# Reordering attention's norm and two in-place sums in a fused attention and feed-forward kernel

## The chip, the cores and the metric

The kernel runs on one core of one Trainium2 chip. The metric is the device time of one execution in microseconds. Five engines work at the same time, each through its own queue: TensorE (PE; PEld is its weight load), VectorE (DVE), ScalarE (ACT), GpSimd (POOL) and SyncE (SP, which here only issues transfers). Matrix products land in PSUM banks; VectorE and ScalarE take them from there.

## The reference

Linear attention without a softmax on 8 batches, 8 heads, 576 tokens and 64 values a head, then a feed-forward block on the 4608 x 512 result:

```
kv  = einsum('bhsd,bhse->bhde', k, v)
out = einsum('bhsd,bhde->bhse', q, kv)
x   = out / sqrt(mean(out*out, -1) + 1e-6) * g_norm      # heads side by side: 4608 x 512
h   = x @ w_in                                           # 512 x 2048
g   = s * max(h, 0)**2 + b
y   = g @ w_out                                          # 2048 x 512
```

Everything is fp32.

## The kernel before

**Units.** The tokens are cut into nine units of 512, u = 0 to 8. In each unit the kernel forms h and g (`mm1`), then y (`mm2`), and between their instructions it computes attention for the next unit, u + 1. Units 0 and 1 have their own forms; units 2 to 8 all use `mm1_deep` and the deep branch of `mm2`. The edits lie in `mm1_deep`, in its inner function `run` (L987).

**Seven products in place of eight.** A matrix product is cut into 2 x 2 blocks and done by Winograd's variant of Strassen's scheme, with seven block products P1 to P7 and sums of blocks ahead of and behind them. One bank takes P1, then P6, P5 and P3 on top of it, and is copied out between them; a second takes P2; a third P7, then P4 on top of it. So a bank's next product can't start until the copy of its contents has been read. The hidden dimension is done in four steps, s = 0 to 3, two to a pair. In `mm1_deep` P1, P5 and P6 are whole products (`x1(s)`, `x5(s)`, `x6(s)`), while P7, P2, P3 and P4 are each cut once more into seven small products: `seven(m)` is the m-th small product of P7 for all four steps at once, and `small(i, pair, m, ...)` are small products of Pi for one pair.

**What follows each product on the other engines.** `seven(5)` is eight matmuls, then a copy of the bank by ScalarE (`keep(4)`, L874), then an add by VectorE (L260) into A22's tile. `seven(3)` goes into the same bank that `keep(4)` has read. `small(i, pair, 5)` is four matmuls, a VectorE add that takes the bank into a tile r (L260) and a second VectorE instruction, `add_relu`, that forms relu of a sum (L267); `small(i, pair, 3)` goes into the bank that r has read. P2 and P3 use the banks `sx_ps` and `z_ps`; P4, being `apart`, uses `st_ps`. `x5(s)` ends with a ScalarE copy (L904), `x6(s)` with another (L861).

**The sums of g's blocks.** `a12(s)` (L906) adds A22's tile to P6's copy, on VectorE for s = 0, 1 and on GpSimd for s = 2, 3. `a22(s)` (L910) is one VectorE instruction of 128 x 512, `add_relu(a22, a22, a21)`, in place. `done(name, steps)` (L982) is ScalarE's part: for each step a square (L984) and a multiply-add by s and b (L652), again in place. `s1` and `s3` add or subtract finished tiles. The functions `p4_34`, `p3_34` and `s1` that `mm2` calls at its start hold the last pieces of the unit's h.

**Attention in the gaps.** `at(n)` in `run` issues what the table `first` of `sides` (L1799) holds for place n. For units 2 to 7: `at(4)` attention's product for the first half of the next unit (A), `at("kv")` the k-v product of a batch in units 4 and 6 (`at("kv3")` in unit 3), `at(5)` A's transposes back from PSUM, its square on ScalarE (L572) and the second half's (B's) first transpose, `at(6)` A's `row_sum` (a VectorE reduction ss of 128 x 1024, L576, and ScalarE's root rms, L580), `at(7)` A's `norm` (VectorE's reciprocal inv, L584, and the multiply xn, 128 x 1024, L586), `at(8)` the transpose of the result. Unit 8 has nothing at these places. `sums_of_xs(4)` (L841) is four VectorE subtractions of 128 x 128.

**What orders the work.** The schedule is written by hand: the program runs in a manual mode, each engine executes its instructions in the order in which the Python code issues them, and semaphores make an instruction wait for the data and buffers that it needs. Weights come through a ring of 14 slots that SP fills; a slot is given back by `used(...)` (L1147) once its product has been issued, and only from the ring's head. q is loaded by POOL's queue (L1727), each tile once attention's norm has read the one before it in its buffer.

Of the kernel before, what the change touches and what calls it, by code (L numbers as in the profile page):

```python
# [17 lines left out]
def kernel(  # L18
# [72 lines left out]
    def matmul(o, lhsT, rhs, start, stop):  # L91
        nc.tensor.matmul(o, lhsT=lhsT, rhs=rhs, start=start, stop=stop, skip_group_check=True)  # L92
# [169 lines left out]
    def sub(o, a, b, engine=nc.vector):  # L262
        engine.tensor_tensor(out=o, in0=a, in1=b, op=ALU.subtract)
# [375 lines left out]
    def bank_of(key, tag, bufs=2):  # L639
        bank[key] = ps_f.tile([P, 2, TB], FP32, name=f"{tag}_ps", tag=tag, bufs=bufs)  # L640
        return bank[key]
# [177 lines left out]
    def mm1_deep(u):  # L819
# [21 lines left out]
        def sums_of_xs(i):  # L841
            x = xs[u, i]
            b11, b12, b21, b22 = (x[:, k, q * P : q * P + P] for k in range(2) for q in range(2))
            t = late["sub"].tile([P, FC // 4, P], FP32, name="sub", tag="sub", bufs=6)
            t1, t2, t3, t4 = (t[:, n] for n in range(4))
            sub(t1, b12, b11)
            sub(t2, b22, t1)
            sub(t3, b22, b12)
            sub(t4, b21, t2)
            for m, x in ((1, b11), (2, b21), (3, b22), (4, t4), (5, t1), (6, t2), (7, t3)):  # L850
                a[i, m] = x
# [11 lines left out]
        def seven(*ms):  # L863

            if ms[0] == 1:
                for t in range(NS):
                    g_tile("a22", t)

            def to(j, h):
                return g_all[0][:, :, j, :, h * P : h * P + P]  # L870

            def keep(n):
                st[7, n] = late["tmp"].tile([P, 2, 2, P], FP32, name="r", tag="q2t" if n == 2 else "q14t")
                nc.scalar.copy(st[7, n], st[7, "x"])  # L874

            for m in ms:
                first = m in (1, 2, 7)
                if first:
                    ps = bank_of(("s", 7, m), "y").rearrange("p b (m c) -> p (b m) c", c=P)
                    st[7, "x" if m == 1 else "y"] = ps.rearrange("p (i b) c -> p i b c", b=2)  # L880
                ps = st[7, "x" if m in (1, 6, 5, 3) else "y"]
                for pair in range(2):
                    w = w_deep(7, pair, m)
                    for b in range(2):
                        matmul(ps[:, pair, b], w[:, b], a[7, m], first and pair + b == 0, True)
                    if m in (7, 3):
                        used((u, (7, pair), 6 if m == 7 else 5))
                if m == 1:
                    keep(1)
                elif m == 2:  # L890
                    add(to(0, 0), ps, st[7, 1])
                elif m == 6:
                    keep(2)
                elif m == 5:
                    keep(4)
                    add(to(1, 1), st[7, "y"], st[7, 4])
                elif m == 3:
                    nc.scalar.copy(to(0, 1), ps)
                elif m == 4:
                    add(to(1, 0), ps, st[7, 2])  # L900
# [9 lines left out]
        def a22(s):  # L910
            add_relu(ga["a22", s], ga["a22", s], ga["a21", s])
# [4 lines left out]
        def s3(s, engine=nc.vector):  # L916
            sub(ga["a21", s], ga["a11", s], ga["a21", s], engine)
# [10 lines left out]
        def small(i, pair, *ms):  # L928
            name = {2: "a11", 3: "a21", 4: "a12"}[i]
            g = (i, pair)  # L930
            apart = i == 4

            def to(j, h):
                return g_pair[name, pair][:, j, :, h * P : h * P + P]

            def bank_for(m):
                if apart:
                    ps = ps_t.tile([P, 2, 2 * P], FP32, name="st_ps", tag="t")
                    return ps[:, 0].rearrange("p (b c) -> p b c", c=P)
                if m == 1:  # L940
                    ps = ps_a.tile([P, DM], FP32, name="sx_ps", tag="x")
                    return ps.rearrange("p (b c) -> p b c", c=P)[:, :2]
                ps = bank_of(("s", m), "z", 1).rearrange("p b (m c) -> p (b m) c", c=P)
                return ps[:, :2]

            def keep(n, j, h):
                if apart:
                    t = late["tmp"].tile([P, 2, 2, P], FP32, name="r", tag="q2t" if n == 2 else "q14t")[:, 0]
                else:
                    t = late["tmp"].tile(  # L950
                        [P, 2, P], FP32, name="r", tag={1: "r14", 2: "r2_2", 4: "q4"}[n]
                    )
                st[g, n] = t
                add(t, st[g, "x"], to(j, h))

            for m in ms:
                first = m in (1, 2, 7)
                if first:
                    st[g, "x" if m == 1 else "y"] = bank_for(m)
                ps = st[g, "x" if m in (1, 6, 5, 3) else "y"]  # L960
                w, x = w_deep(i, pair, m), a[i, m]
                for b in range(2):
                    matmul(ps[:, b], w[:, b], x, first and b == 0, True)
                if m == 7:
                    used((u, g, 6))
                elif m == 3:
                    used((u, g, 5))
                if m == 1:
                    keep(1, 0, 0)
                elif m == 2:  # L970
                    add_relu(to(0, 0), ps, st[g, 1])
                elif m == 6:
                    keep(2, 1, 0)
                elif m == 5:
                    keep(4, 1, 1)
                    add_relu(to(1, 1), st[g, "y"], st[g, 4])
                elif m == 3:
                    add_relu(to(0, 1), ps, to(0, 1))
                elif m == 4:
                    add_relu(to(1, 0), ps, st[g, 2])  # L980

        def done(name, *steps):  # L982
            for s in steps:
                nc.scalar.square(ga[name, s], ga[name, s])  # L984
                affine(ga[name, s])

        def run(at, early):  # L987
            x1(0)
            at(2)
            sums_of_xs(7)  # L990
            seven(1)
            x1(1)
            sums_of_x()
            seven(2)
            small(2, 0, 1, 2)
            x6(0)
            seven(6)
            at(4)
            at(5)
            seven(7)  # L1000
            small(2, 0, 6, 7)
            at("kv")
            x6(1)
            sums_of_xs(4)
            seven(5)
            at(6)
            x5(0)
            at(7)
            small(2, 0, 5)
            seven(3)  # L1010
            small(2, 0, 3, 4)
            seven(4)
            at("kv3")
            a12(0)
            a22(0)
            small(3, 0, 1, 2)
            done("a11", 0, 1)
            at(8)
            x5(1)
            a12(1)  # L1020
            a22(1)
            small(3, 0, 6, 7)
            at(9)
            done("a22", 0)
            at(10)
            x1(2)
            at(11)
            small(3, 0, 5)
            x1(3)
            at(12)  # L1030
            small(3, 0, 3, 4)
            done("a22", 1)
            x6(2)
            a12(2)
            at(13)
            small(4, 0, 1, 2)
            x6(3)
            a12(3)
            done("a21", 0, 1)
            at(14)  # L1040
            small(4, 0, 6, 7)
            small(2, 1, 1, 2)
            s1(0, nc.gpsimd)
            x5(2)
            at(15)
            small(4, 0, 5)
            small(2, 1, 6, 7)
            s1(1, nc.gpsimd)
            x5(3)
            small(4, 0, 3, 4)  # L1050
            small(2, 1, 5)
            s3(0, nc.gpsimd)
            a22(2)
            done("a12", 0, 1)
            small(4, 1, 1, 2)
            small(2, 1, 3, 4)
            s3(1, nc.gpsimd)
            at(16)
            a22(3)
            done("a22", 2)  # L1060
            small(4, 1, 6, 7)
            done("a11", 2, 3)
            small(3, 1, 1, 2)
            early()
            at(18)
            done("a22", 3)
            small(4, 1, 5)
            small(3, 1, 6, 7)
# [777 lines left out]
    for u in range(U):  # L1846
# [16 lines left out]
        for s in range(NS if u > 0 else 0):  # L1863
            a = steps[s]

            def at(n):
                for fn in first.get((s, n), []):
                    fn()
# [75 lines left out]
```

## Time and profile before

| what | value |
|---|---|
| median of 3 runs (lowest to highest) | 914.72 us (914.28 to 917.06) |
| the profiled execution's own time | 914.67 us |
| its span, from first to last instruction | 912.8 us |
| granted TensorE clock | 0.999 of full speed |
| busy: PE, PEld | 890.7 us, 824.0 us |
| busy: DVE, ACT, POOL | 698.4 us, 361.7 us, 313.9 us |
| HBM traffic | 171.71 MB read, 28.31 MB written |

The difference between the profiled time and the span lies around the first and the last instruction. Matmul ends are modelled, so a TensorE stall is better read at PEld, where the timeline gives the idle time ahead of an instruction in brackets, with the engine that ended it. Consecutive instructions of VectorE and ScalarE overlap a little in the records: a duration is from its start to the acknowledged end, and the next one can start some 0.1 us before that. Starts are in microseconds from the start of the span. In the timeline L267 is `add_relu`, the L260 instruction r<-sx_ps,a or r<-st_ps,a is the take-out of a small product, and a tile's name leaves out its number.

Units 2 to 8 begin their `run` at intervals of some 96 to 98 us: `seven(3)` of units 2 to 7 starts on PEld at 253.09, 348.21, 448.92, 546.69, 644.35 and 739.64 us.

### The profile page before, as it was taken

To read this page: it belongs to the slowest core of one execution; us is meant where nothing else is said; L and a number is where in the kernel's file an instruction comes from. 1 tells how busy PE (TensorE), PEld (TensorE's weight loads), DVE (VectorE), ACT (ScalarE), POOL (GpSimd) and SP (SyncE) were. 2 spreads that over 40 slices of the span, in tenths; PEclk is the share of its full clock that TensorE was granted. 3 is DMA by queue.
4 is the path that set the end of the run, shared out by engine and by line. 5 is a ranking of instruction groups with operands and counts; after the bars stand their busy time and mean duration, and the time that the engine had idled before them with its cause. 6 is when DMAs were issued, how large, how long until landed. Compare 5 with 4: busy or idle time off the path is not lost.

```text
span 912.8 us, 20461 instructions
## 1 busy us (share of the span) xinstructions
PE 890.7 (98%) x7874; PEld 824.0 (90%) x7874; DVE 698.4 (77%) x1389; ACT 361.7 (40%) x612; POOL 313.9 (34%) x535
## 2 busy tenths in 40 slices
PE   7999999999999998999999999999999999999998
PEld 4888888888989997999899998999899989999998
DVE  2898778886587967798579867887779777984696
ACT  3887024422267014720365026701671047204710
POOL 2027066024656034732276026803470303021300
PEclk9999999999999999999999999999999999999999
DMA  9898638459945974499538973696649922993386
GB/s 273 301 322 244 191 105 281 167 153 375 320 134 157 315 267 138 145 316 318 187 89 258 319 257 93 183 318 227 209 114 319 294 83 77 296 317 109 82 288 186
DMA packets 128721, 201.39 MB, mean 221 GB/s; under 512 B 26225, under 2 KB 44017, under 8 KB 128625
## 3 DMA queue, kind: packets, MB, share of 16 engines
q1 hardware_dynamic: 108656, 174.23, 59.7%
q0 software_dynamic: 16512, 23.63, 9.1%
q10 hardware_dynamic: 3456, 2.23, 1.0%
q8 instruction: 63, 1.03, 0.5%
q14 instruction: 34, 0.27, 0.1%
HBM read 171.71 MB, written 28.31 MB: 219 GB/s over the span
## 4 chain that ended last, share of the span: by engine, by line
PE 89%; DVE 7%; ACT 1%; DMA 1%; issue 1%; SPq 0%; DVEq 0%; ACTq 0%
PE x_ps L92 44%; PE y_ps L92 22%; PE z_ps L92 10%; PE sx_ps L92 5%; PE st_ps L92 4%; PE y_ps L553 2%; PE kv_ps L385 2%; DVE a L267 1%; DVE xn L586 1%; DMA kv_sb<-in_v_dram 1%; DVE ss L576 1%; DVE r L260 1%; DVE a L260 1%; DVE xT L597 0%; ACT r L874 0%
## 5 line engine op out<-in xcount | busy, mean ns | idle before, releaser
L1727 POOL DMA_DIRECT2D q_sb<-in_q_dram x296 | 166.8, 571 | 90.9 <-issue 63.9
L1306 POOL DMA_DIRECT2D out_dram<-o x120 | 59.4, 502 | 262.2 <-DVE o L260 148.1
L92 PE MATMUL x_ps<-w_sb,sub 128*128 128x128 f32 x1176 | 148.5, 275 | 0.0
L92 PEld LDWEIGHTS x_ps<-w_sb,sub 128*128 128x128 f32 x1176 | 139.8, 192 | 0.0
L652 ACT ACTIVATE a<-a,b_col,s_col 128x512 f32<-128x512 f32 x144 | 117.0, 814 | 27.5 <-DVE a L655 19.2
L856 ACT COPY a<-x_ps 128x512 f32<-128x512 f32 x28 | 16.3, 581 | 244.4 <-PE x_ps L92 244.4
L92 PE MATMUL x_ps<-xs,ws_raw 128*128 128x256 f32 x384 | 91.3, 381 | 0.1
L92 PE MATMUL x_ps<-xT,wa 128*128 128x256 f32 x360 | 84.9, 381 | 0.1
L92 PEld LDWEIGHTS x_ps<-xs,ws_raw 128*128 128x128 f32 x384 | 69.5, 190 | 8.4 <-ACT r L730 0.5
L92 PEld LDWEIGHTS x_ps<-xT,wa 128*128 128x128 f32 x360 | 66.1, 190 | 10.3 <-ACT a L652 1.3
L984 ACT ACTIVATE a<-a 128x512 f32<-128x512 f32 x112 | 69.5, 621 | 14.5 <-DVE a L267 13.7
L92 PE MATMUL x_ps<-w_sb,a 128*128 128x128 f32 (+1 forms) x432 | 64.9, 298 | 0.0
L92 PE MATMUL y_ps<-w_sb,a 128*128 128x128 f32 (+1 forms) x416 | 62.4, 295 | 0.0
L92 PEld LDWEIGHTS x_ps<-w_sb,a 128*128 128x128 f32 x432 | 58.4, 192 | 2.9 <-issue 0.4
L92 PEld LDWEIGHTS y_ps<-w_sb,a 128*128 128x128 f32 x416 | 56.0, 192 | 2.1
L260 DVE TENSOR_TENSOR r<-x_ps,o 128x256 f32<-128x256 f32 (+1 forms) x84 | 29.8, 355 | 28.4 <-PE x_ps L92 27.7
L92 PE MATMUL y_ps<-w_sb,sub 128*128 128x128 f32 x392 | 49.5, 275 | 0.0
L92 PE MATMUL z_ps<-w_sb,a 128*128 128x128 f32 (+1 forms) x352 | 46.9, 280 | 0.0
L92 PEld LDWEIGHTS y_ps<-w_sb,sub 128*128 128x128 f32 x392 | 46.6, 192 | 0.0
L260 DVE TENSOR_TENSOR a<-y_ps,r 128x512 f32<-128x512 f32 x31 | 21.4, 691 | 31.9 <-ACT r L874 15.8
L260 POOL TENSOR_TENSOR a<-a,r 128x512 f32<-128x512 f32 x14 | 17.8, 1271 | 79.2 <-DVE r L260 49.4
L260 DVE TENSOR_TENSOR r<-sx_ps,a 128x256 f32<-128x256 f32 x84 | 35.1, 417 | 11.7 <-PE sx_ps L92 11.1
(234 smaller groups left out, 1820.5 us busy)
## 6 DMA issues: line engine op xcount, KB each, us to landing
w_sb<-w SPq DMA_DIRECT2D x455, 256.0 KB, 5.0
w_sb<-w SPq DMA_DIRECT2D x14, 512.0 KB, 8.2
w<-sub POOLq DMA_DIRECT2D x28, 256.0 KB, 6.2
out_dram<-o POOLq DMA_DIRECT2D x112, 64.0 KB, 4.2
w_sb<-in_k_dram SPq DMA_DIRECT2D x24, 288.0 KB, 5.2
w_sb<-in_v_dram SPq DMA_DIRECT2D x24, 288.0 KB, 5.5
w_raw<-in_moe_w_in_dram SPq DMA_DIRECT2D x6, 1024.0 KB, 7.6
q_sb<-in_q_dram POOLq DMA_DIRECT2D x160, 32.0 KB, 4.2
```

The costliest lines, as they stand in the source:

```text
L92: nc.tensor.matmul(o, lhsT=lhsT, rhs=rhs, start=start, stop=stop, skip_group_check=True)
L260: engine.tensor_tensor(out=o, in0=a, in1=b, op=ALU.add)
L267: nc.vector._custom_dve(TENSOR_ADD_SAT, out=o, in0=a, in1=b, s0=float("inf"), s1=0.0)
L385: nc.tensor.matmul(ps[r][(r ^ l) * HB : (r ^ l) * HB + HB, i, :], lhsT=kv[l][0][rows, j, :], rhs=kv[l][1][rows, j, :], start=(j == 0), sto ...
L553: nc.tensor.matmul(ps[l][32 * p : 32 * p + 32, r, lo:hi], lhsT=bd_kv[b % 2][rows, p, at : at + 32], rhs=st["qT"][rows, p, lo:hi], start=Tr ...
L576: nc.vector.reduce_sum(st["ss"], st["xn"].rearrange("p (h d) -> p h d", d=D), axis=mybir.AxisListType.X)
L586: nc.vector.tensor_tensor(out=st["xn"].rearrange("p (c h e) -> p h c e", c=KC, h=2 * W), in0=q_tile[c].rearrange("p (h c e) -> p h c e", h ...
L652: nc.scalar.activation(t, t, AF.Identity, scale=s_col, bias=b_col)
L856: nc.scalar.copy(g_tile("a11", s), st["x", s])
L984: nc.scalar.square(ga[name, s], ga[name, s])
L1306: queues[s % 2].dma_start(out=view[b, jj, :, cols], in_=st[name, j][s * w : s * w + w, cols])
L1727: load()
```

## The change

Three moves in `run`; no instruction is added, removed or altered.

1. `at(6)` and `at(7)`, A's row sum, root, reciprocal and norm, go ahead of `seven(5)`. Before, `at(6)` stood behind `seven(5)` and `at(7)` behind `x5(0)`.
2. `a22(2)` goes from behind `small(2, 1, 5)` and `s3(0)` to behind `small(4, 1, 1, 2)` and `small(2, 1, 3, 4)`.
3. `a22(3)` goes from ahead of `small(4, 1, 6, 7)` to behind it.

```diff
             at("kv")
             x6(1)
             sums_of_xs(4)
+            at(6)
+            at(7)
             seven(5)
-            at(6)
             x5(0)
-            at(7)
             small(2, 0, 5)
             seven(3)
             small(2, 0, 3, 4)
...
             small(4, 0, 3, 4)
             small(2, 1, 5)
             s3(0, nc.gpsimd)
-            a22(2)
             done("a12", 0, 1)
             small(4, 1, 1, 2)
             small(2, 1, 3, 4)
+            a22(2)
             s3(1, nc.gpsimd)
             at(16)
-            a22(3)
             done("a22", 2)
             small(4, 1, 6, 7)
+            a22(3)
             done("a11", 2, 3)
             small(3, 1, 1, 2)
             early()
             at(18)
             done("a22", 3)
```

The first move acts in units 2 to 7, the other two in units 2 to 8. The order of `done` on ScalarE is untouched.

## The prediction

> **What bounds the kernel now.** I read the page first (engine rows, the chain that ended last), then who waited for whom, then the chain and the timeline around the two edited places in every token unit u = 2 to 8. The span is 912.8 us and the profiled execution took 914.67 us, so 1.87 us lie around the span; the median of the runs shown is 914.72, close enough that one sum serves for both.
>
> ```profile
> PE 890.7 (98%) x7874; PEld 824.0 (90%) x7874; DVE 698.4 (77%) x1389; ACT 361.7 (40%) x612; POOL 313.9 (34%) x535
> ...
> PE 89%; DVE 7%; ACT 1%; DMA 1%; issue 1%; SPq 0%; DVEq 0%; ACTq 0%
> ```
>
> TensorE carries 89% of the chain. A change of order that adds no matmul can win only where another engine holds the chain: VectorE's 7%, ScalarE's 1%. The list of waits says where that is.
>
> ```profile
> PEld sx_ps L92 <- DVE r L260: 12.9, 12, 1.9
> ...
> PEld st_ps L92 <- DVE r L260: 3.5, 14, 0.3
> ```
>
> The first row is six waits of 1.93 us (one each in u = 2 to 7) and six of 0.22 us; the second is 0.31 + 0.18 us in each of seven units. The chain in unit 4 shows what the 1.93 us consist of.
>
> ```profile
> 447.11 0.59 ACT r L874
> ...
> 447.73 0.69 DVE a L260
> 448.42 1.14 DVE ss L576
> ...
> 449.58 0.32 ACT rms L580
> ...
> 449.92 0.26 DVE inv L584
> ...
> 450.21 1.23 DVE xn L586
> 451.43 0.34 DVE r L260
> ...
> 451.82 0.71 PE sx_ps L92 x4
> ```
>
> P7's fifth product is copied by ScalarE (`keep(4)`) and added by VectorE; then attention's row sum, root and norm run, and only then VectorE takes P2's fifth product out of its bank (r), for which TensorE is waiting. But VectorE had nothing to do before that add:
>
> ```profile
> 447.73 0.69 DVE L260 TENSOR_TENSOR a<-y_ps,r 128x512 f32<-128x512 f32 x1 [4.02 <-ACT r L874]
> ...
> 545.49 0.69 DVE L260 TENSOR_TENSOR a<-y_ps,r 128x512 f32<-128x512 f32 x1 [1.55 <-ACT r L874]
> ```
>
> Idle 4.02 us in units 4 and 6, 1.55 us in 3, 5 and 7, and 0.89 us in 2 (its sums of x come late, behind a store).
>
> **What the Trainium skill says.** "PSUM — Partial Sum Buffer", section "Engine vs sequencer instructions": the ScalarE, VectorE and GpSimdE queues are strict FIFO and matmuls stay in program order. The chain above agrees: r starts 0.08 us before the norm's slot ends and not earlier, although its product was done 2 us before. The same page, "PSUM bank collisions raise a hardware error", says to guard a bank by semaphores and not by address, so a product into a bank waits for the reader before it; here TensorE starts 0.05 us after r ends (451.35 + 0.42 = 451.77, 451.82). For ScalarE, "ScalarE: Activation LUTs", section "What ACT_TABLE_LOAD costs", states 280 ns + 0.833 ns an element with a pointer bias; by it the root of 16 elements would take 293 ns, and the trace has 308.
>
> **Part 1: row sum, root, reciprocal and norm ahead of `seven(5)`.** Four instructions move (reduce 1.21, root 0.31, reciprocal 0.25, multiply 1.23 us); they issue no DMA. On VectorE they pass P7's add alone. On ScalarE the root passes `keep(4)`, and queued behind it are the copy of `x5(0)` and, through the bank, TensorE's `seven(3)`. SP and POOL have nothing between the two places.
>
> Units 3, 5, 7, worked in unit 5. The last sum of x starts at 543.66 and that run's spacing is 0.21, so the reduce starts at 543.87 and ends at 545.08; its input (square, 541.62 + 1.06) is ready. Root 0.04 later, 545.12; reciprocal 0.33 after the root's start, 545.45; multiply +0.29, 545.74; P7's add +1.14 (before, the next instruction started 549.11 - 547.97 after the multiply), 546.88; r +0.61 (546.10 - 545.49), 547.49; TensorE +0.48 (549.59 - 549.11), 547.97 in place of 549.59. **Gain 1.62 us**; TensorE, ready at 549.59 - 1.93 = 547.66, still waits 0.31. `keep(4)` goes from 544.88 to 545.33, 0.21 behind the root's start, and ends at 545.92; `seven(3)` wants its bank at 546.69, so 0.77 us cover the new wait.
>
> Units 4 and 6: ScalarE copies `x6(1)` at 446.16 and takes the root one spacing (0.47, as 449.79 to 450.26) later, 446.63. VectorE thus idles 2 us behind its reduce, but nothing that is late is queued there. Reciprocal 446.96, multiply 447.25, add 448.39, r 449.00, or 449.23 when its product is there (448.37 + 0.86, the distance in unit 8). It ends at 449.65; TensorE is ready at 451.82 - 1.93 = 449.89. **Gain 1.93**, the whole wait; TensorE itself is next.
>
> Unit 2: the reduce can start at 250.93 (last sum 250.72 + 0.21); r follows 3.62 us later as in unit 5, 254.55, before 255.52. **Gain 0.97**; `keep(4)` ends at 252.97, just ahead of `seven(3)` at 253.09, so the cover is 0.12.
>
> Sum: 0.97 + 3 x 1.62 + 2 x 1.93 = **9.69 us**. Unit 8 has no attention and shows the same place without the stall. What follows (A12, A22, P3) restarts from TensorE's `seven(4)`, behind which VectorE idles 0.47, so it moves as one. The moved norm also frees a q tile some 3 us earlier in units 4 and 6, and POOL's loads of q then run beside SP's weight loads. I price that at nothing; its upper end is the 0.99 us that unit 3 shows at 358.85, where a weight load issued at 354.3 lands 4.4 us later.
>
> **Parts 2 and 3: A22 of steps 2 and 3 behind the neighbours' products.** Each is one VectorE instruction of 0.68 us, with no DMA; both pass VectorE work only. Unit 8:
>
> ```profile
> 858.12 0.68 DVE L267 CUSTOM_DVE_ANT_0 a<-a,a 128x512 f32<-128x512 f32 x1
> ...
> 858.72 0.42 DVE L260 TENSOR_TENSOR r<-st_ps,a 128x256 f32<-128x256 f32 x1
> ...
> 859.64 0.61 ACT L984 ACTIVATE a<-a 128x512 f32<-128x512 f32 x1
> ...
> 863.30 0.42 DVE L260 TENSOR_TENSOR r<-st_ps,a 128x256 f32<-128x256 f32 x1
> ```
>
> VectorE runs without a gap from 857.32 to 863.3. With the same spacings (0.34 to the next independent one, 0.55 from r to its sum, 0.60 behind a 512-wide one) the new order is r 858.12, a 858.67, two more 859.01 and 859.34, A22(2) 859.67, r 860.27, A22(3) 860.60, r 861.20, and from there as before. TensorE loses its waits of 0.31 and 0.18, and waits instead for the r at 861.20 and the one at 863.30, which have not moved; its product at 863.77 starts when it did. **Gain zero**: the instructions in front of that r are the same ones.
>
> The cost is on ScalarE. It squares and scales one tile after another (1.37 us each) and reaches A22(2) at 859.64; now that comes at 859.67 + 0.68 + 0.03 = 860.38, 0.74 late. Queued behind it are A22(2), A11(2), A11(3), A22(3), A12(2), A12(3), A21(2), A21(3), then the copy of the last matrix product's P1 out of its bank. Gaps of 0.02 and 0.23 on the way give back 0.25, so 0.49 arrive. In unit 4 the two that wait at the end are:
>
> ```profile
> 489.64 0.24 ACT L1181 COPY r<-x_ps 128x128 f32<-128x128 f32 x1
> 489.77 0.69 DVE L260 TENSOR_TENSOR s<-a,a 128x512 f32<-128x512 f32 x1 [0.50 <-ACT a L652]
> ...
> 490.14 0.97 PEld L92 LDWEIGHTS x_ps<-w_sb,sub 128*128 128x128 f32 x8
> ```
>
> The copy would end at 489.64 + 0.49 + 0.24 = 490.37, and the next product into that bank starts 0.06 later (as L730's copy, 139.02, and its product, 139.08): 490.43, TensorE 0.29 late. VectorE's s starts 0.49 late and VectorE then has no gap until 505.64; three TensorE starts (494.60, the second half of the run at 493.71; 497.29; 499.97) have only 0.11, 0.13 and 0.07 us to spare behind its results (ends 494.44, 497.11, 499.85, and 0.05 to pass on). The last makes it 0.49 - 0.07, a loss of **0.42 us** a unit. Bounds: 0, if ScalarE has more slack than I see, to 0.49; I take 0.42 x 7 = **2.94 us**.
>
> **The sum.** 914.67 - 9.69 + 2.94 = 907.92; I forecast **907.9 us**, 0.75% below the median.
>
> **Rivals.** (a) A22's lateness is hidden: 914.67 - 9.69 = 905.0. For it: ScalarE is busy only 40%. Against: the 0.50 us wait quoted above is on just that queue. (b) Part 1's gain is partly given back, because TensorE, early, meets the next late thing (weights, or P3's bank): with half of it, 914.67 - 4.85 + 2.94 = 912.8. For it: unit 3's 0.99 us; against: that wait counts from the kv product, which itself moves. (c) Slower: ScalarE's lag after A22(2) is longer than 0.49 us, because the four evictions now ahead of A22(2) wait themselves for TensorE, and ScalarE and then VectorE and TensorE stand behind it in lockstep. It decides from 9.69 / 7 = 1.4 us a unit; at 2 us it gives 914.67 - 9.69 + 14 = 919.0. Against: their products are done before their slots (the latest at 859.11 for 859.34). (d) That the new order is not what the engines run: not possible, queues follow the program.
>
> **Chances.** Forecast 0.64, with its own range 906.2 to 909.6; (a) 0.18; (b) 0.10; (c) 0.08. About 0.3% (2.7 us) can be told from no change, so faster is below 912.0: forecast, (a) and a small part of (b), 0.84; (b) mostly within, 0.08; slower 0.08. The range, 904.4 to 912.0, takes in (a) with its bounds and stops short of most of (b) and of (c).
>
> **What would show it.** Step by step: the 1.93 us waits on sx_ps fall to about 0.3 us in units 3, 5, 7, to none in 4 and 6, to 0.96 in 2; the reduce directly follows the sums of x; `st_ps` waits change place and not their sum; ScalarE idles about 0.74 us ahead of A22(2)'s square, and a wait of x_ps on ScalarE's copy of some 0.3 us appears seven times. I am wrong if a new wait over 0.5 us a unit stands between `seven(3)` and `small(4,1)`, or if the x_ps wait is missing.

## The result and the profile after

| kernel | median of its runs | lowest to highest | ratio to before, 95% interval |
|---|---|---|---|
| before (same comparison) | 914.91 us | 914.28 to 917.06 | |
| changed | 907.6 us | 907.1 to 909.89 | 0.9921 [0.9897, 0.9945] |

The forecast was 907.9 us with a range of 904.4 to 912.0. The profiled execution of the changed kernel is the slowest of its four, 909.89 us with a span of 908.1; where it lost time is said below. These are the page's engine row and chain, then rows of the list of waits (engine and line, what it waited for: us in total, times, longest).

```profile
PE 892.8 (98%) x7874; PEld 825.3 (91%) x7874; DVE 698.4 (77%) x1389; ACT 362.1 (40%) x612; POOL 313.5 (35%) x535
...
PE 80%; DVE 8%; DMA 5%; issue 4%; POOL 1%; ACT 1%; SPq 0%; DVEq 0%; POOLq 0%; ACTq 0%
```

```profile
PEld sx_ps L92 <- DVE r L260: 6.1, 17, 1.0
...
PEld x_ps L92 <- ACT r L1181: 1.3, 7, 0.2
...
PEld st_ps L92 <- DVE r L260: 0.2, 1, 0.2
```

Busy times are those of before: no work was added or removed. The waits on sx_ps fell from 12.9 to 6.1 us although there are more of them: seven are new, 0.41 us each, ahead of P3's sixth small product of the second pair, and stand where the waits on st_ps (3.5 us) had been, of which one of 0.2 us is left. A new wait of x_ps on ScalarE came seven times, as forecast. The chain's DMA share was 1% before and is now 5%; that is taken up with unit 2. Now the stretch of part 1 in unit 4, in the timeline (start, duration, engine, line, and in brackets the idle time ahead with what ended it):

```profile
443.37 1.21 DVE L576 TENSOR_REDUCE ss<-xn 128x16 f32<-128x1024 f32 x1
...
446.39 0.31 ACT L580 ACTIVATE rms<-ss,eps_col 128x16 f32<-128x16 f32 x1
...
446.74 0.25 DVE L584 RECIPROCAL inv<-rms 128x16 f32<-128x16 f32 x1 [2.15 <-ACT rms L580]
...
448.17 0.68 DVE L260 TENSOR_TENSOR a<-y_ps,r 128x512 f32<-128x512 f32 x1
...
448.98 0.42 DVE L260 TENSOR_TENSOR r<-sx_ps,a 128x256 f32<-128x256 f32 x1
...
449.56 0.53 PEld L92 LDWEIGHTS sx_ps<-xT,w_sb 128*128 128x128 f32 x4
```

The reduction follows the sums of x at once, VectorE waits its 2.15 us for the root (behind the copy of `x6(1)` on ScalarE) where nobody needs it, and P2's third small product starts without a wait. Unit 5 keeps the forecast rest:

```profile
546.65 0.52 PEld L92 LDWEIGHTS sx_ps<-xT,w_sb 128*128 128x128 f32 x4 [0.29 <-DVE r L260]
```

Now the places where the two moved A22 were to cost, in unit 4:

```profile
476.17 0.68 DVE L267 CUSTOM_DVE_ANT_0 a<-a,a 128x512 f32<-128x512 f32 x1
...
476.88 0.63 ACT L984 ACTIVATE a<-a 128x512 f32<-128x512 f32 x1 [0.66 <-DVE a L267]
...
487.84 0.24 ACT L1181 COPY r<-x_ps 128x128 f32<-128x128 f32 x1
487.97 0.69 DVE L260 TENSOR_TENSOR s<-a,a 128x512 f32<-128x512 f32 x1 [0.68 <-ACT a L652]
488.13 0.97 PEld L92 LDWEIGHTS x_ps<-w_sb,sub 128*128 128x128 f32 x8 [0.19 <-ACT r L1181]
```

ScalarE stands idle 0.66 us for A22(2), and 11 us later this lost time shows at its queue's end: VectorE waits longer for ScalarE's last scaled tile (0.68 in place of 0.50 us), and TensorE waits for ScalarE's copy.

Two stretches of TensorE's time account for the difference. The first runs from attention's product at `at(4)` to `x1(2)` (part 1 lies in it), the second from there to the next unit's product (parts 2 and 3); starts are PEld's in the timelines. "Again" is a second profile of the changed kernel, 907.26 us.

| unit | first: before | changed | again | second: before | changed | again |
|---|---|---|---|---|---|---|
| 2 | 17.41 | 17.09 | 16.44 | 77.89 | 78.29 | 78.30 |
| 3 | 20.34 | 19.11 | 18.24 | 77.89 | 78.29 | 78.29 |
| 4 | 19.87 | 17.85 | 17.86 | 80.37 | 81.33 | 80.76 |
| 5 | 17.29 | 15.66 | 15.65 | 77.90 | 78.29 | 78.29 |
| 6 | 19.87 | 17.86 | 17.86 | 77.90 | 78.63 | 78.65 |
| 7 | 17.23 | 15.60 | 15.60 | | | |

The first stretches give 8.84 us in the first profile and 10.36 in the second. The second ones cost 0.40 us, but for unit 6 (0.73 or 0.75) and unit 4 of the first profile. The first profile is 2.7 us longer than the second: 0.64 us were lost ahead of unit 2 (its first stretch starts at 245.82, in the second profile at 245.18), 0.65 in unit 2, 0.87 in unit 3 and 0.57 in unit 4's second stretch. Those of units 2 and 3 are explained below. In unit 4 TensorE stands 0.41 us at a k-v product, for which the profile names no cause; one of the other orders below has the same wait (0.44 us).

### The profile page after: what moved, and what is told of

It is laid out like the page before. It is cut to its first block, busy times and chain, and to the rows that moved or that the text cites. A ratio compares the mean times of both kernels' runs of the same rounds, so it can differ in the third digit from the quotient of the medians.

```text
span 908.1 us, 20461 instructions
## 1 busy us (share of the span) xinstructions
PE 892.8 (98%) x7874; PEld 825.3 (91%) x7874; DVE 698.4 (77%) x1389; ACT 362.1 (40%) x612; POOL 313.5 (35%) x535
## 4 chain that ended last, share of the span: by engine, by line
PE 80%; DVE 8%; DMA 5%; issue 4%; POOL 1%; ACT 1%; SPq 0%; DVEq 0%; POOLq 0%; ACTq 0%
PE x_ps L92 40%; PE y_ps L92 18%; PE z_ps L92 9%; PE sx_ps L92 5%; PE st_ps L92 4%; DMA w<-sub 3%; DVE a L267 2%; PE y_ps L553 2%; PE kv_ps L385 1%; DMA kv_sb<-in_v_dram 1%; DVE xn L586 1%; POOL w L1200 1%; DVE r L260 1%; DVE sub L263 1%; DVE ss L576 1%
## 5 line engine op out<-in xcount | busy, mean ns | idle before, releaser
L92 PEld LDWEIGHTS x_ps<-xT,wa 128*128 128x128 f32 x360 | 66.1, 190 | 10.3 <-ACT a L652 1.3
L92 PEld LDWEIGHTS z_ps<-w_sb,a 128*128 128x128 f32 x352 | 43.4, 192 | 0.4
```

## The experiments

Times are medians with the lowest and highest run; each ratio is against the kernel before on the same chip.

**Part 1 alone.**

```diff
+            at(6)
+            at(7)
             seven(5)
-            at(6)
             x5(0)
-            at(7)
```

> Part 1 alone on the kernel before (row sum and norm ahead of P7's fifth product; both A22 where they were). My theory: the whole gain is part 1's and parts 2 and 3 cost 0.4 us a unit through ScalarE's queue, so this is faster than the changed kernel: 914.8 - 9.7 = 905.1 us (904.3 to 906.5, since unit 2 depends on a store that lands late), and no wait of x_ps on ScalarE's copy r L1181. Rival, the A22 moves are free: about 907.6 us, the same as the changed kernel. Rival, the A22 moves carry part of the gain: above 909 us.

Measured 904.74 us (904.09 to 905.43), ratio 0.9886 [0.9869, 0.9903]; before 915.37. Run again with a later version it gave 904.75, ratio 0.9892 [0.9875, 0.9908]:

> Part 1 alone once more, on the same chip as the version with the sums later, so that the two can be compared: 904.7 us.

Part 1 gives more than the whole change. The list of waits has no row of x_ps on L1181, and its second stretches are those of before (77.89 us in units 2, 3, 5 and 6), so the earlier loads of q, which the prediction priced at nothing, cost nothing there.

**Parts 2 and 3 alone.**

```diff
-            a22(2)
             done("a12", 0, 1)
             small(4, 1, 1, 2)
             small(2, 1, 3, 4)
+            a22(2)
             s3(1, nc.gpsimd)
             at(16)
-            a22(3)
             done("a22", 2)
             small(4, 1, 6, 7)
+            a22(3)
```

> Parts 2 and 3 alone on the kernel before (both A22 late, norm where it was). My theory: slower, 914.8 + 0.42 x 7 = 917.7 us, with seven waits of x_ps on ScalarE's copy of about 0.2 us. Rival, free: 914.8 us. Rival, they help because TensorE's waits on st_ps (0.49 us a unit) go: 914.8 - 3.4 = 911.4 us.

Measured 918.49 us (917.38 to 919.1), ratio 1.0035 [1.0021, 1.0048]: slower, by 3.1 us. ScalarE stands idle 0.66 us ahead of A22(2) as above. The list of waits has, first before and then here:

```profile
DVE s L260 <- ACT a L652: 3.6, 7, 0.5
```

```profile
PEld sx_ps L92 <- DVE r L260: 15.8, 19, 1.9
...
DVE s L260 <- ACT a L652: 6.2, 14, 0.7
...
PEld x_ps L92 <- ACT r L1181: 1.3, 7, 0.2
```

TensorE's waits on st_ps did go, and were worth nothing: seven waits of 0.41 us on sx_ps came for them (19 in place of 12, 15.8 in place of 12.9 us). The rival that counted them as a gain falls.

**Part 3 alone.**

```diff
-            a22(3)
             done("a22", 2)
             small(4, 1, 6, 7)
+            a22(3)
```

> Part 3 alone on the kernel before: only A22 of step 3 goes behind P4's small products 6 and 7. My theory: no effect, 914.8 us (within 0.5), since ScalarE reaches A22(3) three microseconds after VectorE has made it in either order; ScalarE is not idle ahead of A22(2)'s square. Rival, both moves cost alike: 914.8 + 1.5 = 916.3 us. Rival, it helps by TensorE's 0.18 us wait on st_ps: 913.5 us.

Measured 914.96 us (913.59 to 917.11), ratio 0.9999 [0.9989, 1.0009]. The row of s waiting for ScalarE is as before (3.6 us, 7 times). So the price is A22(2)'s. That move was not run by itself, but in the changed kernel too ScalarE has no idle time ahead of A22(3)'s square.

**The changed kernel with ScalarE's order adapted.**

```diff
-            done("a22", 2)
             small(4, 1, 6, 7)
             a22(3)
             done("a11", 2, 3)
+            done("a22", 2)
             small(3, 1, 1, 2)
```

> The changed kernel with one more move: ScalarE squares and scales A11(2) and A11(3) before A22(2), so that it has work while A22(2) isn't made yet. VectorE and TensorE keep the changed kernel's order. My theory, the cost of the A22 moves is ScalarE's idle 0.7 us: it goes, 914.8 - 9.7 = 905.1 us, and x_ps waits no more on ScalarE's copy. Rival, the cost lies in VectorE's or TensorE's new order: 907.6 us, as the changed kernel.

Measured 905.09 us (904.91 to 905.71), ratio 0.989 [0.9876, 0.9904]. VectorE and TensorE have the changed kernel's order, only ScalarE squares A11 while A22(2) is not made. The second stretches of units 2, 3 and 5 are back at 77.89 us, and the time is within 0.4 us of part 1 alone. So the cause of the 0.40 us was ScalarE's idle time and not VectorE's or TensorE's order, and the rival that put it there falls, but for one unit: unit 6 keeps a loss of 0.34 us (78.24).

**A larger dose.** Both A22 go behind P3's first two small products, ScalarE's order kept. Here A22(2) reads A21 of step 2 after P3 has replaced half of its tokens, so it sums other values, in the same instruction and shape.

```diff
-            a22(2)
             s3(1, nc.gpsimd)
             at(16)
-            done("a22", 2)
             small(4, 1, 6, 7)
-            a22(3)
-            done("a11", 2, 3)
             small(3, 1, 1, 2)
+            a22(2)
+            done("a22", 2)
+            a22(3)
+            done("a11", 2, 3)
```

> The changed kernel with a larger dose of parts 2 and 3: both A22 go further back, behind P3's first two small products, and ScalarE keeps its order (A22(2), A11(2), A11(3), A22(3)). My theory: A22(2)'s square starts 2.4 us later than in the kernel before instead of 0.74; of it 0.25 is slack, so about 2.1 us a unit reach TensorE, less what it gains meanwhile on st_ps and sx_ps (at most 0.5): 914.9 - 9.0 + 7 x (1.6 to 2.1) = 917 to 921 us. Rival (the price is a fixed one for the changed order and not ScalarE's idle time): 907.6 us, as the changed kernel.

Measured 920.8 us (919.86 to 923.5), ratio 1.0066 [1.0052, 1.008], at the top of what was expected. A22(2)'s square comes 2.62 us later than before in place of 2.4, and the second stretch is 80.16 us, 2.27 longer than before in place of 1.6 to 2.1. The expected relief of up to 0.5 us on st_ps did not come; instead the take-out of P4's fifth small product was late as well.

```profile
480.58 0.63 ACT L984 ACTIVATE a<-a 128x512 f32<-128x512 f32 x1 [2.53 <-DVE a L267]
482.74 0.52 PEld L92 LDWEIGHTS st_ps<-xs,w_sb 128*128 128x128 f32 x4 [1.45 <-DVE r L260]
...
491.82 0.97 PEld L92 LDWEIGHTS x_ps<-w_sb,sub 128*128 128x128 f32 x8 [1.41 <-ACT r L1181]
```

ScalarE's idle time of 0, 0.66 and 2.53 us goes with a loss of 0, 0.40 and 2.27 us a unit: about 0.25 us is free, the rest is paid in full. Unit 6 of the changed kernel fits between them, with 1.01 us idle and 0.73 lost.

**Half of part 1: the row sum and its root alone.**

```diff
+            at(6)
             seven(5)
-            at(6)
             x5(0)
             at(7)
```

> Half of part 1 on the kernel before: the reduction and the root go ahead of P7's fifth product, the reciprocal and the norm's multiply stay behind x5(0). My theory (what counts is VectorE work shifted into its idle time): by the same spacings the take-out r comes 0.48 us earlier in unit 2, 1.12 in units 3, 5 and 7, and 1.57 in 4 and 6, sum 6.98 us: 914.9 - 7.0 = 907.9 us. Rival (the gain comes from the norm's end, which frees the q tile for the next loads, or from the multiply alone): the norm ends hardly earlier, so below a third of part 1's 9.7 us: above 911.7 us.

Measured 907.84 us (906.71 to 908.88), ratio 0.9924 [0.9911, 0.9937]; before 914.8. The waits that are left in units 2, 3 and 4 are those that the spacings give (1.93 - 0.48 would have been 1.45, 1.93 - 1.12 = 0.81, 1.93 - 1.57 = 0.36), but for unit 2, where the sums of x did not come late this time:

```profile
255.12 0.52 PEld L92 LDWEIGHTS sx_ps<-xT,w_sb 128*128 128x128 f32 x4 [0.82 <-DVE r L260]
...
349.07 0.52 PEld L92 LDWEIGHTS sx_ps<-xT,w_sb 128*128 128x128 f32 x4 [0.76 <-DVE r L260]
...
447.84 0.52 PEld L92 LDWEIGHTS sx_ps<-xT,w_sb 128*128 128x128 f32 x4 [0.33 <-DVE r L260]
```

Two thirds of part 1's gain are there. By itself this does not exclude the rival of the q tile, whose expectation was wrong in one point: the multiply does end earlier than before, by 1.16 us in unit 5 and 1.59 in unit 4, the very times by which r comes earlier. What speaks against the rival is where the gain lies. With part 1 alone the wait on sx_ps in unit 5, which ends with r each time, falls from 1.93 to 0.29 us, and the first stretch is 1.64 us shorter; here the wait falls to 0.76 and the stretch is 1.16 us shorter. So the gain is this wait, which leaves nothing for q: VectorE's work moved into VectorE's idle time.

**The changed kernel again.**

> The changed kernel once more, for its spread. If unit 2's small gain in the first profile (0.3 us in place of 0.97) hangs on when a store of weights lands, the idle time of VectorE ahead of the sums of x in unit 2 differs from the 1.30 us of that profile, and the 0.5 us wait of P7's third product on ScalarE's copy with it; time 907 to 910 us. If it is built into the new order, both come back as they were.

Measured 907.71 us (907.26 to 908.29), ratio 0.9922 [0.9907, 0.9937]. First a line of unit 2 in the profile before, then the lines of the first profile of the changed kernel, then of this one:

```profile
249.98 0.29 DVE L263 TENSOR_TENSOR sub<-xs 128x128 f32<-128x128 f32 x1 [0.63 <-DMA w<-sub]
```

```profile
251.16 0.29 DVE L263 TENSOR_TENSOR sub<-xs 128x128 f32<-128x128 f32 x1 [1.30 <-DMA w<-sub]
...
254.18 0.97 PEld L92 LDWEIGHTS y_ps<-xs,w_sb 128*128 128x128 f32 x8 [0.50 <-ACT r L874]
```

```profile
249.86 0.29 DVE L263 TENSOR_TENSOR sub<-xs 128x128 f32<-128x128 f32 x1 [0.65 <-DMA w<-sub]
...
254.89 0.52 PEld L92 LDWEIGHTS sx_ps<-xT,w_sb 128*128 128x128 f32 x4 [0.97 <-DVE r L260]
```

The sums of x in unit 2 wait for a buffer that a store of unit 1's weight sums still reads. When that store lands late, the root comes late, `keep(4)` stands behind it on ScalarE, and P7's third product waits 0.50 us. This time it landed as in the profile of before, and unit 2 gained 0.97 us. In the first profile of part 1 alone it held nothing up, and unit 2 gained 1.52 us.

**Two versions meant to beat both.** First, the sums of x between row sum and norm:

```diff
+            at(6)
             sums_of_xs(4)
+            at(7)
             seven(5)
-            at(6)
             x5(0)
-            at(7)
```

> A version meant to beat both: part 1 alone, and the four sums of x (sums_of_xs(4), needed only some 20 us later) go between the row sum and the norm, where VectorE waits for the root. My theory: the remaining 0.3 us wait in units 3, 5 and 7 goes, and unit 2's chain doesn't start behind the late store any more (its keep(4) doesn't delay P7's third product): 0.9 + 1.0 to 1.5 us below part 1 alone, so 902.4 to 903.2 us. Rival (the store still holds VectorE ahead of the norm in unit 2, and the rest is bound elsewhere): 904.7 us, as part 1 alone.

Measured 903.73 us (903.12 to 904.18), ratio 0.9876 [0.9863, 0.9889]; its interval overlaps that of part 1 alone. The 0.29 us waits went (first stretches 15.28 and 15.22 us in units 5 and 7), but not unit 2's: there the store held the sums for 0.95 us, now between row sum and norm, and TensorE waited 0.80 us. The version's own expectation overlooked that the norm stands behind them in the same queue. So the sums had to leave the stretch:

```diff
-            sums_of_xs(4)
+            at(6)
+            at(7)
             seven(5)
-            at(6)
             x5(0)
-            at(7)
...
             at(12)
+            sums_of_xs(4)
             small(3, 0, 3, 4)
```

> Part 1 alone, and the four sums of x (needed for P4's small products) go out of this stretch, behind the second half's row sum at at(12), where VectorE waits 0.35 us for a root and then has 0.46 us to spare. So nothing stands between the square and the row sum. My theory: unit 2's wait, which kept 0.8 us when the sums stood between row sum and norm and waited there for a store (idle 0.95 us), goes as well as the 0.3 us waits of units 3, 5 and 7; at(12) hides the moved sums: 914.9 - 9.7 - 0.9 - 1.0 = 903.3 us. Rival (the row sum in unit 2 waits for something else, or the sums cost 0.5 us a unit at their new place): unit 2 keeps its wait, 904.7 us or more.

Measured **902.89 us** (902.42 to 903.66), ratio 0.9868 [0.9853, 0.9883], with part 1 alone at 904.75 on the same chip. Unit 2's first stretch falls to 15.38 us, and the list has no sx_ps wait at this place in any unit:

```profile
249.46 1.20 DVE L576 TENSOR_REDUCE ss<-xn 128x16 f32<-128x1024 f32 x1
...
251.39 0.25 DVE L584 RECIPROCAL inv<-rms 128x16 f32<-128x16 f32 x1 [0.73 <-ACT rms L580]
```

```profile
PE 92%; DVE 4%; DMA 2%; ACT 1%; issue 1%; ACTq 0%; DVEq 0%
```

The second stretch stays at 77.89 us, so the sums cost nothing at their new place, and TensorE now carries 92% of the chain.

## Why the prediction was right

**Part 1** was forecast at 9.69 us; alone it measured 10.6 and 10.3 us (915.37 to 904.74, 915.02 to 904.75), and the changed kernel's first stretches gave 10.36 and 8.84. Units 5 and 7 were forecast at 1.62 and gave 1.63 or 1.64, with 0.29 us left where 0.31 was expected; units 4 and 6 were forecast at 1.93 and gave 2.01 or 2.02, the whole wait and 0.08 us more. Relative to the stretch's start VectorE's and ScalarE's instructions hit to 0.05 us in units 4 and 5. So the mechanism and its sizes stand.

**Unit 2** was the term that was not fixed: forecast 0.97, measured 0.97 in one profile and 0.32 in the other, so that the hit in the second is luck with one store. The prediction gave `keep(4)` a cover of 0.12 us there without saying what its loss would bring; a store 0.65 us later used it up. **Unit 3** moved by 1.23 and 2.10 in place of 1.62, because its wait at `small(3, 0, 6)`, which the prediction put down to a late weight load, was 0.99 us before, 1.40 in the first profile and 0.53 in the second. The profile before names an add of VectorE as what ended it, but in the second profile the product starts at 356.04, ahead of that add's end at 356.49. In the first profile the chain names the load:

```profile
353.24 4.85 DMA w_sb<-w
358.09 0.14 issue
358.23 0.68 PE sx_ps L92 x4
```

No run moved the load.

**Parts 2 and 3** were forecast at 0.42 us a unit, 2.94 in all. Alone they measured 3.1 us, the stretches 0.40 in most units, and part 1 alone lies 2.9 us below the changed kernel. VectorE's new order came to 0.01 us as worked out, and A22(2)'s square was 0.74 us late as forecast. The lateness reached TensorE on the forecast path: in unit 4, against before and relative to the start of `x1(2)`, ScalarE's last tile made s 0.47 us late, TensorE was 0.26 late behind the copy, and 0.40 late at the third of the three starts that the prediction named:

```profile
498.10 1.86 PEld L92 LDWEIGHTS x_ps<-w_sb,sub 128*128 128x128 f32 x16
```

Before, it stood at 499.97. The prediction charged both moves together; the price is A22(2)'s alone. TensorE's start into L1181's bank came 0.05 us after the copy's end (487.84 + 0.24 = 488.08, 488.13), as the price of 0.06 had it; the wait itself is 0.19 us in place of some 0.3. That TensorE's earlier starts on st_ps would be lost again was right to the hundredth: P4's third small product starts at 480.27 for 482.54, 2.27 us earlier than before, as `x1(2)` is (456.45 for 458.72). Unit 6 pays 0.35 us more in the changed kernel, with parts 2 and 3 alone and with ScalarE's order adapted, but not with the larger dose (80.16 us as elsewhere). There the prediction's argument against rival (c), that the products are done before their slots, does not hold, since a take-out ahead of A22(2) waits for TensorE:

```profile
668.65 0.42 DVE L267 CUSTOM_DVE_ANT_0 a<-st_ps,r 128x256 f32<-128x256 f32 x1 [0.49 <-PE sx_ps L92]
```

ScalarE then stands idle 1.01 us in place of 0.66. Why only in this unit stays open.

Of the rivals, (a), A22's lateness hidden, did not come in the changed kernel; the adapted order on ScalarE makes it true, at 905.09 where 905.0 was worked out. (b) came only in unit 3 of the first profile, which gave 0.39 of 1.62 us back at the weight load. (c) showed in unit 6 as said; its point of 1.4 us a unit was passed only by the larger dose, which did end slower than before.

The measured 907.6 us lies in the range, and the gain of 0.8% is clear of its interval, which ends at 0.9945. That the median came within 0.3 us of 907.9 is partly luck, since units 2 and 3 alone differ by 1.5 us between the two profiles, and unit 6's extra cost was not in the sum.

## What to carry to other kernels

Before moving an instruction, look at the idle time ahead of it and ahead of what it displaces: here work put into a gap of its own engine shortened the path, while work moved behind others on a full engine gained nothing and made the next engine wait. An engine that is busy 40% over the span can be full for 12 us, as ScalarE was, and a gap in such a run was paid at its end, less the slack between: the price followed ScalarE's idle time and vanished, but for unit 6, when ScalarE got other work for that moment. If an early step is put behind one that can wait for a transfer, the path takes over that transfer's changes from one execution to the next, as in unit 2; put the step that depends on memory traffic elsewhere.

## What was not expected

The chain in the first profile of the changed kernel runs through unit 1's stores (DMA 5% and issue 4%, where before it had 1% each), because the moved norm had joined the critical chain to VectorE instructions that wait for them. In unit 2 the chain goes from a store through the sums of x, the row sum and the norm to TensorE:

```profile
244.04 7.10 DMA w<-sub
...
252.18 1.14 DVE ss L576
...
256.18 0.71 PE sx_ps L92 x4
```

The landing of this store moved VectorE's idle time in unit 2 from 0.63 to 1.30 us between executions of kernels with the same work.
